# One iteration more between making Z's operands and summing Z, in the attention stage of a fused forward and backward kernel

## The chip, the cores and the metric

The kernel runs on one core of one Trainium2 chip. The metric is device time in microseconds (us) of one execution; the time of a kernel is the median of its runs. The engines are called by the names that the profile uses: PE is TensorE (PEld its weight loads), DVE is VectorE, ACT is ScalarE, POOL is GpSimd, SP is SyncE, whose queue issues most transfers.

## The reference

The kernel computes the output and all gradients of a block with attention and a gated MLP on x of 2048 x 512, with 32 heads of 16:

```python
x = A_x
xn = _layernorm(x, axis=-1)
s = _A_ref(xn, A_wqkv, A_wo)
g = _silu(_B_ref(xn, B_w1, B_b1, B_w2, B_b2))
return x + s * g
```

and in `_A_ref`

```python
scores = jnp.einsum("bhqd,bhkd->bhqk", q, k) * (Dh ** -0.5)
p = _softmax(scores, axis=-1)
o = jnp.einsum("bhqk,bhkd->bhqd", p, v)
```

Outputs are this result and, by `jax.vjp` with a given `grad_out`, the gradients of x, wqkv, wo, w1, b1, w2 and b2. The change lies in the attention stage, where the forward of the softmax and the gradients of q, k and v are made together.

## The kernel before, in words

A first stage (`Pre`) computes the layer norms, the projections and the MLP. The attention stage (`attention_core`) follows, then the rest of the gradients (`Grads.run`). The order of instructions on every engine is written out by hand: an engine works in the order in which the code emits to it, and tiles in pools with few buffers add waits.

The attention stage works on 64 blocks, j = 0 to 63: 16 pairs of heads by 4 chunks of 512 queries (`qc`). A block has 16 iterations, one for every 128 keys (`kb`), and the loop variable g counts all 1024 of them. "Iteration 4" is g % 16 == 4. One iteration emits, among others:

- `emit_d` (L1137): for both heads, the product of the output's gradient with v, `d`, into one of three PSUM buffers; `emit_s` (L1115): the scores `s` of the next iteration, into one double bank; `emit_exp` (L1124, ACT): their exponential into `ets`, a ring of 11 places.
- `emit_z(g + ZOFF)` (L1334): four matmuls of Z, the gradients of k and v, of a block whose first pass lies some iterations back.
- `emit_x` (L1232, L1235, L1239): three groups of four matmuls into X, the sums over keys; the group at L1239 reads `gts` of the iteration before.
- `emit_T` (L1192, L1196): transposes of the exponentials of the iteration before into `tT`; `emit_cT` (L1208, ACT) and `emit_cO` (L1215, DVE) copy them to `ek`, the operand of later Z.
- `emit_mult` (L1155, DVE): two products d * exp, one for each head, into `gts`. A gts buffer holds two iterations, so a new one is opened in the even ones. POOL copies one piece of `ets` beside them (L1153). In the odd iterations `emit_dmat` has SP transpose the buffer by DMA into `gk`, the other operand of Z.

When a block has ended, `emit_xs` (L1248, DVE) takes X out in iteration 0 of the next, `emit_XT` transposes it on PE in iterations 1 and 6, `emit_xt` (L1274) and `emit_fin` take it further on DVE and POOL in 2 and 7, and make the weights W of Z. Z of the block then runs through the following 16 iterations, in two halves (`kp`) of eight:

```python
def z_unit(g):
    j = g // 16
    m = g % 8
    return (j, (g % 16) // 8, m if m < 4 else 7 - m, m // 4) if 0 <= j < NB else None
```

The first four of a half read `gk` and W2, the last four `ek` and W1. Each half is summed in one PSUM bank, and after its eighth iteration `emit_acc` (L1346, L1348, DVE) adds it to `acc`; the next half can begin only when that is done. `emit_acc` stands between the two products of an iteration:

```python
for hj in range(2):
    nc.vector.tensor_tensor(out=gts[:, kb % 2, 4 * hj:4 * hj + 4, :], ...)
    if hj == 0:
        emit_xs(g - 1)
        emit_acc(g + ZOFF)
```

At the last query chunk of a pair POOL casts acc to `ob` (L1352) and issues its two stores (L1355). After the last block the loop goes on for -ZOFF iterations in which only Z is left; `tail_mid` puts the first projections of the next stage (L584, L586, L591, L575) into the third and fourth of them.

Of the kernel before, what the change touches and what calls it, by code (L numbers as in the profile page):

```python
# [1050 lines left out]
def attention_core(ctx, ctx_r, tc, k, grads, Oall, dQall, dKVT_out, ident_f32, ident_bf, npairs=16, nqc=4):  # L1051
# [67 lines left out]
    def emit_exp(g):  # L1119

        a = a_unit(g)
        if a is None:
            return
        nc.scalar.activation(out=st_et[g].rearrange("k b h q -> k h b q"),  # L1124
                             in_=cur["s"][:].rearrange("k h (b q) -> k h b q", b=4), func=ACT.Exp)
# [15 lines left out]
    def emit_mult(g):  # L1141
        a = a_unit(g)
        if a is None:
            emit_xs(g - 1)
            emit_acc(g + ZOFF)
            return
# [7 lines left out]
        for hj in range(2):  # L1154
# [3 lines left out]
# [4 lines that stand above are left out]
# [55 lines left out]
    def emit_x(g, part):  # L1217
        a = a_unit(g)
        if a is None:
            return  # L1220
        j, kb = a
        if part == "e" and kb == 0:
            blk[j]["X"] = ps_x.tile([128, 512], f32, name="X", tag="X")
        X = blk[j]["X"]
        NATt = op_of(j)["NAT"]
        et = st_et[g]
        for c in range(4):
            half, hj = c // 2, c % 2
            r = 32 * c
            ev = et[:, half::2, hj, :]  # L1230
            if part == "e":
                nc.tensor.matmul(X[r:r + 32, 0:256], lhsT=NATt[:, kb, hj, 1:33], rhs=ev,  # L1232
                                 start=(kb == 0), stop=False, skip_group_check=True, tile_position=(0, r))
            elif part == "l":
                nc.tensor.matmul(X[r:r + 32, 256:512], lhsT=Lc[:], rhs=ev,  # L1235
                                 start=False, stop=False, skip_group_check=True, tile_position=(0, r))
            else:
                gv = st_gt[g][:, kb % 2, 4 * hj + half:4 * hj + 4:2, :]
                nc.tensor.matmul(X[r:r + 17, 256:512], lhsT=NATt[:, kb, hj, 0:17], rhs=gv,  # L1239
                                 start=False, stop=(kb == 15), skip_group_check=True, tile_position=(0, r))  # L1240

    def emit_xs(g):
        a = a_unit(g)
        if a is None or a[1] != 15:
            return
        j = a[0]
        xs = xsp.tile([128, 512], f32, name="xs", tag="xs")
        nc.vector.tensor_copy(out=xs[:], in_=blk[j].pop("X")[:])  # L1248
        blk[j]["xs"] = xs
# [66 lines left out]
    def emit_z(g):  # L1316
        u = z_unit(g)
        if u is None:
            return
        j, kp, qb, part = u  # L1320
        if part == 0 and qb == 0:
            blk[j]["Z"] = ps_z.tile([128, 512], f32, name="Z", tag="z")
        Z = blk[j]["Z"]
        for par in range(2):
            kc = 2 * kp + par
            for hj in range(2):
                r = 64 * par + 32 * hj
                if part == 0:
                    mv = blk[j]["Gk"][kc][:, :, 4 * hj + qb, :]
                elif 2 * qb + hj == 7 * (1 - par):  # L1330
                    mv = blk[j]["Gk"][kc][:, :, 8, :]
                else:
                    mv = blk[j]["Ek"][kc][:, :, 2 * qb + hj - par, :]
                nc.tensor.matmul(Z[r:r + 32, :], lhsT=WT[j % 2][1 - part][:, qb, hj, :], rhs=mv,  # L1334
                                 start=(part == 0 and qb == 0), stop=(part == 1 and qb == 0), tile_position=(0, r))

    def emit_acc(g):
        u = z_unit(g)
        if u is None or u[2] != 0 or u[3] != 1:
            return  # L1340
        j, kp = u[0], u[1]
        p, qc = blocks[j]
        Z = blk[j]["Z"]
        av = acc[:, kp, :]
        if qc == 0:
            nc.vector.tensor_copy(out=av, in_=Z[:])  # L1346
        else:
            nc.vector.tensor_tensor(out=av, in0=Z[:], in1=av, op=ALU.add)  # L1348
        if qc == nqc - 1:
            ob = (outp.tile([128, 512], bf16, name="ob") if kp == 0 or j < NB - 1 else  # L1350
                  xsp.tile([128, 512], bf16, name="ob", tag="xs"))
            nc.gpsimd.tensor_copy(out=ob[:], in_=av)  # L1352
            dv = dKVT_out[p * 64:(p + 1) * 64, :].rearrange("r (a b s) -> r a b s", a=2, b=2)
            for b in range(2):
                nc.gpsimd.dma_start(out=dv[:, kp, b, :], in_=ob[b * 64:(b + 1) * 64, :])  # L1355

    FIN_AT = {1: 1, 6: 0}
    FIN_END = {1: 1, 2: 0}
    ZOFF = -20
    late = []  # L1360
    for hj in range(2):
        emit_s(0, hj)
    emit_exp(0)
    for g in range(NSTEP - ZOFF):
        cur["g"] = g
# [20 lines left out]
        emit_exp(g + 1)  # L1386
        emit_z(g + ZOFF)
        emit_x(g - 1, "e")
# [28 lines left out]
def full_kernel(ctx, tc, A_x, A_wqkv, A_wo, B_x, B_w1, B_b1, B_w2, B_b2, grad_out,  # L1417
# [35 lines left out]
    with ExitStack() as cO, tc.manual_schedule():  # L1453
        op0p = cO.enter_context(tc.tile_pool(name="op0", bufs=1, side="right", reuse_waits="tile"))
        k.op0 = make_op(nc, op0p, 0)
        k.Lc = op0p.tile([128, 32], bf16, name="Lc")
        nc.gpsimd.memset(k.Lc[:], 0.0)
        nc.gpsimd.memset(k.Lc[:, 17:18], 1.0)
        op0p.tile([128, 96], mybir.dt.uint8, name="pad_to_256r")
        kv, nat, q, do, natd = op_loads(k, k.op0, 0, nc.sync.dma_start)  # L1460
        first = dict(kv=kv, q=lambda: (nat(), q()), do=lambda g: (do(g * 512, g * 512 + 512), natd(g * 4, g * 4 + 4)))
        with ExitStack() as cP:
            Pre(cP, tc, k, first, A_x, A_wqkv, A_wo, B_w1, B_b1, B_w2, B_b2, grad_out)
        pO = cO.enter_context(tc.tile_pool(name="persistO", bufs=1, reuse_waits="tile"))
        k.Oall = pO.tile([128, NT, D], bf16, name="Oall", tag="Oall")
        k.dQall = pO.tile([128, NT, D], bf16, name="dQall", tag="dQall")
        grads = Grads(cO, tc, k, pO, op0p, A_x, grad_out, A_wqkv, A_wo, B_w1, B_w2,
                      (out_0, out_1, out_2, out_3, out_4, out_5, out_6, out_7))
        with ExitStack() as cB:
            attention_core(cB, cB.enter_context(ExitStack()), tc, k, grads, k.Oall, k.dQall, k.dKVT_s, k.ident_f, k.ident_bf)  # L1470
        grads.run()
# [56 lines left out]
```

## Time and profile before

| what | value |
|---|---|
| median of 3 runs | 2180.5 us (2179.21 to 2181.51) |
| profiled execution, time | 2180.46 us |
| profiled execution, span | 2178.8 us |
| granted TensorE clock, mean | 0.997 |
| busy: PE, DVE, ACT, POOL | 2133.0, 1898.0, 1782.2, 870.6 us |
| products of d and exp (L1155, DVE) | 2048, 682 ns each |
| exponentials (L1124, ACT) | 1024, 1027 ns each |
| sums of Z (L1348 and L1346, DVE) | 96 and 32, 681 ns each |
| Z matmuls (L1334, PE) | 4096, 389 ns each |

Time is counted in the profile from the start of the span. The attention stage takes from about 218 to 1841 us. Four matmuls of one group that go to different parts of the array run side by side, so their durations are not to be added; their starts tell more than their ends.

### The profile page before, as it was taken

How to read it: one execution, taken by the hardware profiler on the slowest of the kernel's cores; microseconds unless marked ns; L12 is line 12 of the kernel's file. 1: busy time of each engine (PE TensorE's matmuls, PEld its weight loads, DVE VectorE, ACT ScalarE, POOL GpSimd, SP SyncE). 2: the span in 40 equal slices, each digit the busy share in tenths (PEclk: the TensorE clock that was granted, in tenths of full speed). 3: DMA queues.
4: the chain of work that ended last, by engine and by line, in shares of the span. 5: the costliest groups of instructions: out<-in, count | busy, mean ns of one | idle time of the engine just before them, and what ended most of it. 6: DMA issues, size and time to landing. Idle time of an engine off the chain costs nothing.

```text
span 2178.8 us, 74934 instructions
## 1 busy us (share of the span) xinstructions
PE 2133.0 (98%) x30659; PEld 1170.6 (54%) x30659; DVE 1898.0 (87%) x3523; ACT 1782.2 (82%) x2481; POOL 870.6 (40%) x2397
## 2 busy tenths in 40 slices
PE   6999999999999999999999999999999999899999
PEld 3444555555555555555555555555555555444444
DVE  6677899999999999999999999999999998788647
ACT  5664899999999999999999999999999997775224
POOL 4376434343434444343434344444434343511003
PEclk9999999999999999999999999999999999999999
DMA  7786999999999999999999999999999999999975
GB/s 235 248 281 202 205 199 198 209 195 200 208 204 198 209 201 201 202 200 206 203 199 201 202 203 201 204 203 204 200 202 206 194 213 212 294 251 240 246 209 178
DMA packets 1416569, 461.17 MB, mean 212 GB/s; under 512 B 1329118, under 2 KB 1400414, under 8 KB 1416224
## 3 DMA queue, kind: packets, MB, share of 16 engines
q1 hardware_dynamic: 1401920, 425.44, 100.3%
q0 software_dynamic: 12720, 29.37, 4.9%
q8 instruction: 240, 3.93, 0.8%
q10 hardware_dynamic: 1584, 1.57, 0.2%
q14 instruction: 105, 0.86, 0.1%
HBM read 62.79 MB, written 64.75 MB: 59 GB/s over the span
## 4 chain that ended last, share of the span: by engine, by line
PE 94%; DVE 2%; DMA 1%; ACT 1%; POOL 0%; issue 0%; SPq 0%; DVEq 0%; ACTq 0%; POOLq 0%
PE tT L1192 22%; PE Z L1334 15%; PE d L1137 15%; PE X L1239 6%; PE X L1232 5%; PE X L1235 5%; PE s L1115 3%; PE ps_dy L909 2%; PE ps_dw L742 2%; PE ps_dw L983 2%; PE ps_h L352 2%; PE ps_m L367 2%; PE ps_dh L875 2%; PE tT L1266 1%; PE ps_dxa L1027 1%; PE ps_dwkv L827 1%
## 5 line engine op out<-in xcount | busy, mean ns | idle before, releaser
L1155 DVE TENSOR_TENSOR gts<-d,ets 128x512 bf16<-128x512 f32 x2048 | 1302.2, 682 | 18.2 <-PE d L1137 3.9
L1124 ACT ACTIVATE ets<-s 128x1024 bf16<-128x1024 f32 x1024 | 1051.6, 1027 | 15.2 <-PE d L1137 3.9
L1208 ACT COPY ek<-tT 128x448 f32<-128x448 f32 (+1 forms) x1024 | 525.1, 513 | 115.0 <-PE tT L1192 31.3
L1192 PE MATMUL tT<-ident_bf,ets 128*128 128x128 bf16 x6790 | 557.9, 221 | 0.0
L1192 PEld LDWEIGHTS <-ets 128*128 128x128 bf16 x6790 | 382.5, 98 | 210.5 <-issue 195.2
L1137 PE MATMUL d<-QDT,KVT 32*128 32x512 bf16 x2048 | 469.4, 384 | 0.0
L1153 POOL COPY gts<-ets 128x128 bf16<-128x128 bf16 x1024 | 281.6, 297 | 387.5 <-ACT ets L1124 382.7
L1115 PE MATMUL s<-QDT,KVT 32*128 32x512 bf16 x2048 | 401.1, 379 | 2.4 <-ACT ets L1124 2.4
L1334 PE MATMUL Z<-gk,W 128*32 128x512 bf16 x2304 | 302.9, 389 | 1.4 <-DVE acc L1348 1.3
L1239 PE MATMUL X<-gts,NAT 128*17 128x256 bf16 x4096 | 290.6, 273 | 0.0
L1232 PE MATMUL X<-ets,NAT 128*32 128x256 bf16 x4096 | 290.4, 273 | 0.0
L1235 PE MATMUL X<-ets,Lc 128*32 128x256 bf16 x4096 | 290.3, 273 | 0.0
L1334 PEld LDWEIGHTS <-W 128*32 128x32 bf16 x4096 | 105.5, 93 | 238.2 <-issue 225.0
L1137 PEld LDWEIGHTS <-KVT 32*128 32x128 bf16 x2048 | 148.5, 91 | 114.3 <-issue 21.5
L1334 PE MATMUL Z<-ek,W 128*32 128x512 bf16 x1792 | 203.6, 389 | 0.0
L1235 PEld LDWEIGHTS <-Lc 128*32 128x32 bf16 x4096 | 110.1, 97 | 108.6
L1215 DVE COPY ek<-tT 128x64 f32<-128x64 f32 x378 | 84.9, 225 | 89.5 <-ACT ek L1208 76.0
L1404 POOL COPY tick<-gts 1x2 bf16<-1x2 bf16 x205 | 36.0, 175 | 313.5 <-DVE gts L1155 313.5
L1115 PEld LDWEIGHTS <-KVT 32*128 32x128 bf16 x2048 | 142.7, 91 | 12.3 <-issue 6.4
L1239 PEld LDWEIGHTS <-NAT 128*17 128x17 bf16 x4096 | 114.7, 91 | 15.4 <-issue 1.1
L1232 PEld LDWEIGHTS <-NAT 128*32 128x32 bf16 x4096 | 108.8, 96 | 5.1 <-issue 5.1
L1295 POOL TENSOR_TENSOR W<-NATQq,rL 128x128 bf16<-128x128 bf16 x64 | 25.5, 399 | 147.9 <-DVE rL L1294 110.3
(252 smaller groups left out, 2470.4 us busy)
## 6 DMA issues: line engine op xcount, KB each, us to landing
gk<-gts SPq DMA_TRANSPOSE x512, 5.6
H1T_s<-h1r SPq DMA_DIRECT2D x28, 256.0 KB, 4.2
HGT_s<-hgT SPq DMA_DIRECT2D x8, 896.0 KB, 4.5
DH_s<-stg SPq DMA_DIRECT2D x12, 512.0 KB, 3.3
hch<-DH_s SPq DMA_DIRECT2D x12, 512.0 KB, 4.8
gp<-H1T_s SPq DMA_DIRECT2D x9, 512.0 KB, 6.8
out_dram<-ob_w POOLq DMA_DIRECT2D x36, 128.0 KB, 4.6
NAT_s<-NS SPq DMA_DIRECT2D x4, 1056.0 KB, 6.1
```

What stands on the lines that cost most here:

```text
L1115: nc.tensor.matmul(s[:, hj, :], lhsT=op["KVT"][r:r + 32, kb * 128:(kb + 1) * 128], rhs=op["QDT"][r:r + 32, qc * 512:(qc + 1) * 512], start ...
L1124: nc.scalar.activation(out=st_et[g].rearrange("k b h q -> k h b q"), in_=cur["s"][:].rearrange("k h (b q) -> k h b q", b=4), func=ACT.Exp)
L1137: nc.tensor.matmul(d[:], lhsT=op["KVT"][r:r + 32, kb * 128:(kb + 1) * 128], rhs=op["QDT"][r:r + 32, qc * 512:(qc + 1) * 512], start=True, ...
L1153: nc.gpsimd.tensor_copy(out=gts[:, kb % 2, 8, :], in_=st_et[g][:, b // 2, b % 2, :])
L1155: nc.vector.tensor_tensor(out=gts[:, kb % 2, 4 * hj:4 * hj + 4, :], in0=st_d.pop((g, hj))[:].rearrange("k (b q) -> k b q", b=4), in1=st_et ...
L1192: nc.tensor.transpose(tb[:, i - cut(g), :], et[:, b // 2, b % 2, :], ident_bf[:])
L1208: nc.scalar.copy(out=blk[j]["Ek"][kb // 4][:, kb % 4, c:7].rearrange("q i k -> q (i k)").bitcast(f32), in_=st_T[g][:, 0:(7 - c) * 64])
L1215: nc.vector.tensor_copy(out=blk[g // 16]["Ek"][kk // 4][:, kk % 4, i].bitcast(f32), in_=st_T[g][:, 448:512])
L1232: nc.tensor.matmul(X[r:r + 32, 0:256], lhsT=NATt[:, kb, hj, 1:33], rhs=ev, start=(kb == 0), stop=False, skip_group_check=True, tile_positi ...
L1235: nc.tensor.matmul(X[r:r + 32, 256:512], lhsT=Lc[:], rhs=ev, start=False, stop=False, skip_group_check=True, tile_position=(0, r))
L1239: nc.tensor.matmul(X[r:r + 17, 256:512], lhsT=NATt[:, kb, hj, 0:17], rhs=gv, start=False, stop=(kb == 15), skip_group_check=True, tile_pos ...
L1334: nc.tensor.matmul(Z[r:r + 32, :], lhsT=WT[j % 2][1 - part][:, qb, hj, :], rhs=mv, start=(part == 0 and qb == 0), stop=(part == 1 and qb = ...
```

## The change

One constant moves by one:

```diff
     FIN_AT = {1: 1, 6: 0}
     FIN_END = {1: 1, 2: 0}
-    ZOFF = -20
+    ZOFF = -21
     late = []
```

`emit_z(g + ZOFF)` and `emit_acc(g + ZOFF)` then belong to an iteration one later. Z of a block began in iteration 4 of the block after it and begins in 5; its two sums were emitted in iterations 11 and, one block later, 3, and are emitted in 12 and 4. In these iterations the sum stands between the two products as before. The loop has one iteration more at its end. Nothing else in the text of the kernel changes; tiles, buffers and the amount of work are the same.

## The prediction

> **What bounds the kernel now.** I read the page first, then the groups of instructions by line, then the timeline of one block of the attention stage, engine by engine. The page:
>
> ```profile
> PE 2133.0 (98%) x30659; PEld 1170.6 (54%) x30659; DVE 1898.0 (87%) x3523; ACT 1782.2 (82%) x2481; POOL 870.6 (40%) x2397
> DVE  6677899999999999999999999999999998788647
> PE 94%; DVE 2%; DMA 1%; ACT 1%; POOL 0%; issue 0%; SPq 0%; DVEq 0%; ACTq 0%; POOLq 0%
> ```
>
> TensorE is busy 98% of the span and carries 94% of the chain that ended last, so nothing looks left to win from another engine. But matmul ends are modelled, and a matmul held up inside its group of four is not told as idle. What the four engines do to each other has to be read from starts. The groups that matter, from the view of groups by line:
>
> ```profile
> L1155 DVE TENSOR_TENSOR gts<-d,ets 128x512 bf16<-128x512 f32 x2048 | 1302.2, 682 | 18.2 <-PE d L1137 3.9 <-ACT ets L1124 1.1 <-POOL tick L1404 1.0
> L1348 DVE TENSOR_TENSOR acc<-Z,acc 128x512 f32<-128x512 f32 x96 | 65.4, 681 | 2.9 <-PE Z L1334 2.9
> L1352 POOL CAST ob<-acc 128x512 bf16<-128x512 f32 x32 | 19.7, 616 | 27.6 <-DVE acc L1348 27.6
> L1355 POOL DMA_DIRECT2D dKVT_s<-ob x64 | 35.8, 562 | 9.6 <-POOL ob L1352 9.5 <-issue 0.2
> ```
>
> 2048 products are two per iteration, in 1024 iterations. I write D4 for the start of the first d matmul in iteration 4 of a block, m0(4) and m1(4) for its two products, T(5) for the transposes and s(5) for the score matmuls issued in iteration 5, and exp(5) for the exponential issued in iteration 4 and read in 5. Block 31 on TensorE, iterations 4 and 5 and the start of 6 (columns: start, length, line, count):
>
> ```profile
> 1010.80 0.39 PE L1137 MATMUL d<-QDT,KVT 32*128 32x512 bf16 x1
> 1010.84 0.39 PE L1115 MATMUL s<-QDT,KVT 32*128 32x512 bf16 x2
> ...
> 1011.17 0.40 PE L1334 MATMUL Z<-gk,W 128*32 128x512 bf16 x4
> ...
> 1011.61 0.40 PE L1239 MATMUL X<-gts,NAT 128*17 128x256 bf16 x4
> 1011.95 0.56 PE L1192 MATMUL tT<-ident_bf,ets 128*128 128x128 bf16 x7
> 1012.45 0.38 PE L1137 MATMUL d<-QDT,KVT 32*128 32x512 bf16 x1
> 1012.45 0.39 PE L1115 MATMUL s<-QDT,KVT 32*128 32x512 bf16 x2
> ...
> 1012.77 0.40 PE L1334 MATMUL Z<-gk,W 128*32 128x512 bf16 x4
> ...
> 1013.21 0.28 PE L1239 MATMUL X<-gts,NAT 128*17 128x256 bf16 x4
> 1013.43 0.56 PE L1192 MATMUL tT<-ident_bf,ets 128*128 128x128 bf16 x7
> ...
> 1013.98 0.39 PE L1137 MATMUL d<-QDT,KVT 32*128 32x512 bf16 x1
> ```
>
> In iteration 5 the transposes start 0.66 after Z, and the four X matmuls that read gts take 0.28. In iteration 4 they take 0.40 and the transposes start 0.78 after Z: TensorE lost 0.12 inside that group. What it waited for is on VectorE and ScalarE:
>
> ```profile
> 1009.80 0.68 DVE L1155 TENSOR_TENSOR gts<-d,ets 128x512 bf16<-128x512 f32 x1
> 1010.40 0.68 DVE L1348 TENSOR_TENSOR acc<-Z,acc 128x512 f32<-128x512 f32 x1
> 1011.00 0.68 DVE L1155 TENSOR_TENSOR gts<-d,ets 128x512 bf16<-128x512 f32 x1
> ```
>
> ```profile
> 1009.76 1.03 ACT L1124 ACTIVATE ets<-s 128x1024 bf16<-128x1024 f32 x1
> ...
> 1011.33 1.03 ACT L1124 ACTIVATE ets<-s 128x1024 bf16<-128x1024 f32 x1
> ...
> 1012.98 1.03 ACT L1124 ACTIVATE ets<-s 128x1024 bf16<-128x1024 f32 x1
> ...
> 1014.54 1.02 ACT L1124 ACTIVATE ets<-s 128x1024 bf16<-128x1024 f32 x1
> ```
>
> VectorE steps on every 0.60 when it is behind. The sum of Z (acc) stands between the two products of iteration 3, so m1(3) starts at 1011.00, one step later than it could, and X and T of the next iteration wait for it: T(4) starts 1011.95 - 1011.00 = 0.95 after m1(3). ScalarE closes the second ring: exp(4) at 1009.76 ends at 1010.79 and s(4) starts 0.05 later, at 1010.84; and exp starts 0.53 after D (1011.33 - 1010.80, 1012.98 - 1012.45), or 0.48 after s where s is late. An exp, its wait and the next s are 1.03 + 0.05 + 0.48 = 1.56, so a block of 16 can hardly be shorter than 25.0: little is to be had here, and a wait of TensorE is partly made up where the exp would have held s anyway.
>
> **The change part by part.** No work is added or removed: the same matmuls of Z, 64 x 2 sums, casts and stores. Everything that hangs on `ZOFF` goes one iteration later.
>
> *Out of iterations 3 and 11.* Iteration 3 keeps its length: acc(3) delays only T(4). In 4 the 0.12 goes: T(4) at 1011.17 + 0.66 = 1011.83, and with the 0.50 from T to D (1011.95 to 1012.45) D5 is 1012.33 instead of 1012.45.
>
> *Into iteration 4.* VectorE would be free at 1010.40 + 0.60 = 1011.00, but m0(4) has to wait for d(4), and then what counts is how soon after D it starts. In even iterations the product opens a new gts buffer, and in the order of the built program it waits for four things there (PE, a DMA queue, ACT, POOL); in odd ones for two. The trace has both cases with VectorE idle, an even one in iteration 4 of block 1 (where no sum stands in 3) and the odd iteration 5 of block 31:
>
> ```profile
> 251.85 0.38 PE L1137 MATMUL d<-QDT,KVT 32*128 32x512 bf16 x1
> ```
>
> ```profile
> 252.43 1.29 DVE L1155 TENSOR_TENSOR gts<-d,ets 128x512 bf16<-128x512 f32 x2 [0.16 <-POOL gts L1153]
> ```
>
> ```profile
> 1012.93 1.29 DVE L1155 TENSOR_TENSOR gts<-d,ets 128x512 bf16<-128x512 f32 x2
> ```
>
> Even: 0.58 after D. Odd: 1012.93 - 1012.45 = 0.48. I take 0.58, from the same iteration and the same four waits; before the change this is hidden in iteration 4, because VectorE comes there late from the sum. After such an idle time the next start is 0.61 later (1.29 less the 0.68 of one product). So m0(4) = 1010.80 + 0.58 = 1011.38, acc at 1011.99, m1(4) at 1012.59, T(5) = 1013.54. Without the wait T(5) would be at 1013.39 or so (exp(5) ends 1012.36, s 1012.41, Z 0.32 later, T 0.66 after it), so m1 decides. T(5) has one transpose more, 0.55 to the next D (1013.43 to 1013.98): D6 = 1014.09 against 1013.98, **+0.11**. Z(5) needs acc(4), over at 1011.99 + 0.68 = 1012.67, before Z's own 1012.73; if it were late, up to 0.15 would vanish under m1. With 0.48, D6 would be 1013.99, +0.01.
>
> The Trainium skill (VectorE: DVE Perf Modes, "The DRAIN you can't avoid") says of chained VectorE copies that a semaphore costs nothing extra. Taken as a rule for these waits it gives the odd value in the even iteration too; the two rows of this trace are 0.10 apart and speak against it here.
>
> *What stays of it.* Before, s(6) waited for exp(6) until 1012.98 + 1.03 + 0.05 = 1014.06, that is 0.08 after D6. After, it starts with D6 at 1014.09: only 0.03 later. But exp(7) starts 0.53 after D6, at 1014.62 against 1014.54: 0.08 later. From there the delay runs on in turns of 0.03 and 0.08, and iteration 12 gets about 0.08.
>
> *Iterations 12 and 13*, where the same happens with the rows
>
> ```profile
> 1023.39 0.38 PE L1137 MATMUL d<-QDT,KVT 32*128 32x512 bf16 x1
> ...
> 1023.78 0.40 PE L1334 MATMUL Z<-gk,W 128*32 128x512 bf16 x4
> ...
> 1024.49 0.56 PE L1192 MATMUL tT<-ident_bf,ets 128*128 128x128 bf16 x7
> ...
> 1026.55 0.39 PE L1137 MATMUL d<-QDT,KVT 32*128 32x512 bf16 x1
> ```
>
> ```profile
> 1025.53 1.03 ACT L1124 ACTIVATE ets<-s 128x1024 bf16<-128x1024 f32 x1
> ```
>
> T(12) gives back 0.05 (0.71 after Z instead of 0.66), but D12 is at 1023.47, m0(12) at 1024.05, m1(12) at 1025.26, T(13) at 1026.21, D14 at 1026.76 against 1026.55: +0.21. s(14) came at 1025.53 + 1.03 + 0.05 = 1026.61 and now comes with D14, +0.15; exp(15), 0.53 after D14, +0.21. The block ends between the two, **+0.18**. From iteration 14 on the sums are the same as before, so the next block starts with this shift and adds its own.
>
> *Elsewhere in the block.* Z itself is four matmuls in every iteration either way. W is written in iteration 2, read now from 5 instead of 4. SP's gk transposes in 1 and 9 now follow a Z of the same iteration, but they wait for m1 of that iteration anyway, which is later than Z. On POOL the cast of ob waits for the sum; behind it stand its two stores and the copies into gts. That runs one iteration later in 32 places; the copies are read by the gk transposes and by nothing on the ring, so I cost it at nothing. Without that cover it is a cast and two issues, 0.62 + 2 x 0.56 = 1.7, in one place per pair.
>
> *The end of the stage.* The first two projections of the tail are issued at fixed iterations, so one of them goes past the sum:
>
> ```profile
> 1845.99 0.68 DVE L1348 TENSOR_TENSOR acc<-Z,acc 128x512 f32<-128x512 f32 x1
> 1846.59 0.68 DVE L586 TENSOR_TENSOR dm_all<-ps_so,s1g 128x512 bf16<-128x512 f32 x1
> ...
> 1847.18 0.68 DVE L591 TENSOR_TENSOR t<-ps_so,s1g 128x512 f32<-128x512 f32 x1
> ```
>
> ```profile
> 1846.72 0.62 PE L1334 MATMUL Z<-gk,W 128*32 128x512 bf16 x8 [0.29 <-DVE acc L1348]
> ```
>
> The last block's Z waits for this sum, and the two products at 1846.59 and 1847.18 now stand ahead of it: two steps of 0.60, **+1.2**, once.
>
> *The sum.* 62 blocks have both sums: 62 x 0.18 = 11.2, with the tail 12.4. The profiled execution took 2180.46 (span 2178.8), practically the median of 2180.5, so the forecast is 2180.5 + 12.4 = 2193.
>
> **The rivals.** *Both waits of X vanish.* The sums leave the stretch of iterations 0 to 3, where xs, its transposed half and the sum pile up on VectorE, and T(4) and T(12) get their 0.12 and 0.05 back: 62 x 0.17 = 10.5 less the tail's 1.2, 2171. For it: VectorE really is idle before m0(4) after the change. Against it: T(5) is free only if m1(4) starts by 1013.39 - 0.95 = 1012.44, so m0(4) by 1011.23, 0.43 after D; the earliest start in the rows is 0.48. That 0.43 is the point that decides. Chance 0.10.
>
> *The four waits cost no more than two.* If they are worked off before d is ready, m0 starts 0.48 after D: D6 +0.01, D14 at 1026.58, +0.03, at most 0.03 a block and 0.02 on the mean of its two turns: 1.2, with the tail 2.4, 2183. For it stands the rule of the skill named above; against it the row at 252.43. Chance 0.14.
>
> *The exps take nothing up.* Then 0.11 and the second wait's own 0.13 stay, 0.24 a block: 14.9 + 1.2, 2197. I hold this for the upper half of the forecast. If POOL's 1.7 came onto the ring in 16 pairs, 27 more; nothing in the waits shows POOL there, 0.03 within the slower cases.
>
> **How the numbers follow.** What a measurement can tell from no change is about 0.2%, 4.4 us. Slower by more: the forecast with its upper case, 0.76. Within: 0.14. Faster: 0.10. The forecast's own range is 2188 to 2199; to hold 8 in 10 it reaches down to 2182, taking in most of the second rival, and up to 2203 for a larger share of the delay.
>
> **What would show it.** Right: in an iteration 5 the X matmuls on gts long (0.4 or more) and T 0.8 after Z, the same in 13; none in 4 and 12; m0(4) and m0(12) 0.58 after D behind an idle VectorE; blocks about 0.18 longer; in the tail Z some 1.2 later behind acc. Wrong: m0(4) at 0.48 or earlier, or T(5) 0.66 after Z.

## Result and profile after

The changed kernel takes 2192.59 us, the median of 6 runs (2190.12 to 2198.02), beside 2180.85 (2177.54 to 2182.04) for 6 runs of the kernel before. The ratio is 1.0059, 95% interval 1.0045 to 1.0073: 11.7 us slower between the medians. A ratio, here and below, is estimated from all runs of both kernels and can differ a little from that of the two medians. The profiled execution after took 2194.41 us, span 2192.7.

The page after, TensorE's share and the two groups that answer to those of before:

```profile
PE 2148.5 (98%) x30659; PEld 1175.7 (54%) x30659; DVE 1896.9 (87%) x3523; ACT 1786.7 (81%) x2481; POOL 870.6 (40%) x2397
L1155 DVE TENSOR_TENSOR gts<-d,ets 128x512 bf16<-128x512 f32 x2048 | 1302.6, 683 | 52.1 <-POOL gts L1153 20.4
L1239 PE MATMUL X<-gts,NAT 128*17 128x256 bf16 x4096 | 296.4, 273 | 0.0
```

Every engine has the same instructions as before; a page alone would say that TensorE became busier by 15 us. The second line tells more: VectorE stands idle before the products for 52.1 us instead of 18.2. The view of VectorE's waits within the attention stage puts the new ones down as follows (us in total, times, longest):

```profile
DVE gts L1155 <- POOL gts L1153: 20.4, 61, 0.3
DVE gts L1155 <- PE s L1115: 18.3, 60, 0.3
```

About 60 times each, that is once a block: the first is m0(12), the second m0(4). In the list of before each of them stands once, with 0.2 us, because VectorE came to these two products late there. The name behind the arrow is that of the semaphore event that came last, which need not be what held the product: before m0(12) POOL's copy ends 0.38 after D (median), earlier than VectorE is done with waiting for d (0.43, see below). The timeline of block 31 on TensorE, iterations 4 and 5, then 12 and 13, with the start of the iteration behind (block 30 started at 986.90 and block 31 at 1012.32):

```profile
986.90 0.38 PE L1137 MATMUL d<-QDT,KVT 32*128 32x512 bf16 x1
...
1012.32 0.38 PE L1137 MATMUL d<-QDT,KVT 32*128 32x512 bf16 x1
...
1018.67 0.38 PE L1137 MATMUL d<-QDT,KVT 32*128 32x512 bf16 x1
...
1019.02 0.39 PE L1334 MATMUL Z<-ek,W 128*32 128x512 bf16 x2
...
1019.47 0.28 PE L1239 MATMUL X<-gts,NAT 128*17 128x256 bf16 x4
1019.68 0.56 PE L1192 MATMUL tT<-ident_bf,ets 128*128 128x128 bf16 x7
1020.18 0.39 PE L1137 MATMUL d<-QDT,KVT 32*128 32x512 bf16 x1
...
1020.61 0.40 PE L1334 MATMUL Z<-gk,W 128*32 128x512 bf16 x4
...
1021.05 0.43 PE L1239 MATMUL X<-gts,NAT 128*17 128x256 bf16 x4
1021.42 0.56 PE L1192 MATMUL tT<-ident_bf,ets 128*128 128x128 bf16 x7
...
1021.97 0.39 PE L1137 MATMUL d<-QDT,KVT 32*128 32x512 bf16 x1
1021.97 0.39 PE L1115 MATMUL s<-QDT,KVT 32*128 32x512 bf16 x2
...
1031.36 0.38 PE L1137 MATMUL d<-QDT,KVT 32*128 32x512 bf16 x1
...
1033.31 0.40 PE L1334 MATMUL Z<-gk,W 128*32 128x512 bf16 x4
...
1034.10 0.56 PE L1192 MATMUL tT<-ident_bf,ets 128*128 128x128 bf16 x7
...
1034.65 0.39 PE L1137 MATMUL d<-QDT,KVT 32*128 32x512 bf16 x1
```

VectorE in the same block (the bracket is the idle time ahead and who ended it):

```profile
1019.26 0.69 DVE L1155 TENSOR_TENSOR gts<-d,ets 128x512 bf16<-128x512 f32 x1 [0.31 <-PE s L1115]
1019.87 0.68 DVE L1348 TENSOR_TENSOR acc<-Z,acc 128x512 f32<-128x512 f32 x1
1020.47 1.88 DVE L1155 TENSOR_TENSOR gts<-d,ets 128x512 bf16<-128x512 f32 x3
...
1031.94 0.69 DVE L1155 TENSOR_TENSOR gts<-d,ets 128x512 bf16<-128x512 f32 x1 [0.34 <-POOL gts L1153]
```

The X group in iteration 4 is back at 0.28 and T follows Z by 0.66 there; in iteration 5 X takes 0.43 and T follows Z by 0.81, in iteration 13 by 0.79. The wait of X has not gone, it has moved one iteration on and grown.

Medians over all blocks, from D to the next D in ns (columns are iterations of a block):

| | 0 | 3 | 4 | 5 | 6 | 7 | 12 | 13 | 14 | 15 | block, us |
|---|---|---|---|---|---|---|---|---|---|---|---|
| before | 1596 | 1570 | 1646 | 1538 | 1614 | 1550 | 1602 | 1556 | 1594 | 1504 | 25.220 |
| after | 1552 | 1584 | 1510 | 1789 | 1538 | 1612 | 1550 | 1734 | 1537 | 1558 | 25.423 |

The block length is that of the third query chunk. There the difference is 0.20; in the other chunks it is 0.20 to 0.22, except in the first chunk of every second pair, where it is 0.08 (25.582 against 25.499). The mean over the 62 blocks is 0.19. From the start of block 1 to the start of block 63 the attention stage is 12.0 us longer in the one profiled execution than in the other, 1581.2 against 1569.2 us. The difference of the medians is in the blocks.

### The profile page after: what moved, and what is told of

It reads as the page before. It is cut to its first block, busy times and chain, and to the rows that moved or that the text cites. A ratio compares the mean times of both kernels' runs of the same rounds, so it can differ in the third digit from the quotient of the medians.

```text
span 2192.7 us, 75058 instructions
## 1 busy us (share of the span) xinstructions
PE 2148.5 (98%) x30659; PEld 1175.7 (54%) x30659; DVE 1896.9 (87%) x3523; ACT 1786.7 (81%) x2481; POOL 870.6 (40%) x2397
## 3 DMA queue, kind: packets, MB, share of 16 engines
q10 hardware_dynamic: 1584, 1.57, 0.2%
## 4 chain that ended last, share of the span: by engine, by line
PE 93%; DVE 2%; DMA 2%; ACT 1%; SPq 1%; POOL 0%; issue 0%; DVEq 0%; ACTq 0%; POOLq 0%
PE tT L1192 22%; PE d L1137 15%; PE Z L1334 15%; PE X L1239 6%; PE X L1232 5%; PE X L1235 5%; PE s L1115 3%; PE ps_dy L909 2%; PE ps_dw L983 2%; PE ps_dw L742 2%; PE ps_h L352 2%; PE ps_m L367 2%; PE ps_dh L875 2%; PE tT L1266 1%; PE ps_qkv L210 1%; PE ps_dxa L1027 1%
## 5 line engine op out<-in xcount | busy, mean ns | idle before, releaser
L1155 DVE TENSOR_TENSOR gts<-d,ets 128x512 bf16<-128x512 f32 x2048 | 1302.6, 683 | 52.1 <-POOL gts L1153 20.4
L1137 PE MATMUL d<-QDT,KVT 32*128 32x512 bf16 x2048 | 475.5, 384 | 0.0
L1239 PE MATMUL X<-gts,NAT 128*17 128x256 bf16 x4096 | 296.4, 273 | 0.0
L1137 PEld LDWEIGHTS <-KVT 32*128 32x128 bf16 x2048 | 152.7, 90 | 114.3 <-issue 21.4
L1115 PEld LDWEIGHTS <-KVT 32*128 32x128 bf16 x2048 | 147.1, 90 | 13.8 <-issue 5.1
```

What stands on the lines that cost most here:

```text
L1115: nc.tensor.matmul(s[:, hj, :], lhsT=op["KVT"][r:r + 32, kb * 128:(kb + 1) * 128], rhs=op["QDT"][r:r + 32, qc * 512:(qc + 1) * 512], start ...
L1137: nc.tensor.matmul(d[:], lhsT=op["KVT"][r:r + 32, kb * 128:(kb + 1) * 128], rhs=op["QDT"][r:r + 32, qc * 512:(qc + 1) * 512], start=True, ...
```

## The experiments

The theory: in iterations 4 and 12 the product m0 is no longer hidden behind a late VectorE, and its four waits, worked off one after another once d is there, set its start; acc, m1, T and the next D follow at fixed distances. The rivals: the sum of Z costs what it costs wherever it stands with VectorE's time in the iteration (then the four waits do not matter); or something other than the sums, which hangs on the same constant, makes the difference.

**The waits taken off the product (first_touch).** A tiny write into the new gts buffer takes over the waits for the buffer's earlier readers and can be worked off while d is still being computed:

```diff
         nc.gpsimd.tensor_copy(out=gts[:, kb % 2, 8, :], ...)
+        if kb in (4, 12):
+            nc.vector.memset(gts[:, 0, 0, 0:1], 0.0)
         for hj in range(2):
```

> The changed kernel with one tiny VectorE write (128x1) into the new gts buffer ahead of the first product of iterations 4 and 12, so that the waits for POOL and the transposes are worked off while VectorE is idle, and the product waits for PE and ACT alone. Theory (the four waits set when the product starts): m0(4) and m0(12) start about 0.49 after D instead of 0.59, T(5) and T(13) each 0.10 earlier, blocks 0.15 to 0.20 shorter, 2181 to 2184. Rival (the place of the sum sets it, whatever it waits for): m0 stays at 0.58, 2192 to 2193.

It took 2182.64 us (2176.63 to 2185.94) beside 2179.23 for the kernel before: ratio 1.0009, interval 0.9998 to 1.0019, clear of the 1.0045 to 1.0073 of the change alone. Block 30 on TensorE, its start, its iteration 4, and the start of block 31 (lines behind the new statement are shifted by two):

```profile
980.93 0.38 PE L1137 MATMUL d<-QDT,KVT 32*128 32x512 bf16 x1
...
987.28 0.38 PE L1137 MATMUL d<-QDT,KVT 32*128 32x512 bf16 x1
...
989.22 0.40 PE L1336 MATMUL Z<-gk,W 128*32 128x512 bf16 x4
...
1006.15 0.38 PE L1137 MATMUL d<-QDT,KVT 32*128 32x512 bf16 x1
```

and on VectorE:

```profile
987.52 0.06 DVE L1155 MEMSET gts<- 128x1 bf16 x1
987.76 0.69 DVE L1157 TENSOR_TENSOR gts<-d,ets 128x512 bf16<-128x512 f32 x1 [0.19 <-PE s L1115]
988.37 0.68 DVE L1348 COPY acc<-Z 128x512 f32<-128x512 f32 x1
988.97 1.28 DVE L1157 TENSOR_TENSOR gts<-d,ets 128x512 bf16<-128x512 f32 x2
```

With one instruction *more* on VectorE, m0(4) starts 0.48 after D instead of 0.59, iteration 5 is 1679 ns instead of 1789, iteration 13 is 1636 instead of 1734, and the block is 1006.15 - 980.93 = 25.22 long, as before the change. The trace also records VectorE's own semaphore instructions, which the page does not count as busy. Ahead of m0(4), medians over the blocks in ns after D:

| | first ends | second starts | second ends | product starts |
|---|---|---|---|---|
| after | 447 | 495 | 545 | 589 |
| first_touch | 434 | none | none | 478 |

The product starts 44 ns behind the last of them in both. In the changed kernel the first waits for PE alone and ends 0.45 after D; the second waits for a DMA queue and ACT, the product itself for POOL. The exponential (ACT) is over 0.02 before D and POOL's copy 0.34 after it, so the waits for these two are met before the first instruction ends. The second instruction still runs for 50 ns, and with the gap ahead of it costs 98 ns, all of it on the way to m0. Ahead of m0(12) the changed kernel has two as well: the first, which waits for d, ends at 433, the second at 531, and the product follows at 575. Over the whole execution VectorE has 1425 such instructions in the changed kernel and 1299 here, 126 fewer, which is two in each of 63 blocks. The Trainium skill (Perfetto Trace Analysis, "Identifying Dependency Chains") says that an instruction which waits for several engines may get semaphore instructions ahead of it. The trace agrees, and adds a price: 98 ns for one of them that stands behind the last arrival on an idle engine.

**Most sums left out, with both constants (few_after, few_before).** If something other than the sums hangs on the constant, the two stay apart.

```diff
-        if qc == 0:
+        if qc == nqc - 1:
             nc.vector.tensor_copy(out=av, in_=Z[:])
-        else:
-            nc.vector.tensor_tensor(out=av, in0=Z[:], in1=av, op=ALU.add)
```

> The changed kernel with three of four sums of Z left out (only the sum of the last query chunk of a pair is made, as a copy, so dK and dV hold one chunk alone). Theory (the sum between the products is all that costs): 46 of 62 blocks lose the 0.20 that the change brought and a few hundredths more, 2178 to 2181, within 1.5 of the kernel before with the same sums left out. Rival (something else that hangs on the constant costs: Z beside eight transposes in 5 and 13, SP's or POOL's waits): it stays 6 to 12 above that kernel.

> The kernel before with three of four sums of Z left out (dK and dV hold one chunk alone). 96 sums of 0.68 go, 65 us of VectorE. Theory (the ring of s and exp takes up most of a wait of TensorE): at most 0.05 to 0.10 in 46 blocks, 2176 to 2179. Rival (VectorE's load or the waits of 0.12 and 0.05 are fully on the path): 46 x 0.17 = 8, 2173 or below.

2177.96 us (ratio 0.9995, 0.9985 to 1.0004) and 2177.84 (0.9994, 0.9983 to 1.0005): the same, as far as runs can tell that spread over 10 us. Block 30, which has no sum in either, on TensorE with the constant of after

```profile
981.32 0.38 PE L1137 MATMUL d<-QDT,KVT 32*128 32x512 bf16 x1
...
1006.46 0.38 PE L1137 MATMUL d<-QDT,KVT 32*128 32x512 bf16 x1
```

and with that of before:

```profile
979.01 0.38 PE L1137 MATMUL d<-QDT,KVT 32*128 32x512 bf16 x1
...
1004.16 0.38 PE L1137 MATMUL d<-QDT,KVT 32*128 32x512 bf16 x1
```

25.14 and 25.15. The blocks that keep one of the two sums differ. Where it stands in 4 or 3, they take 25.297 against 25.227 in one half of the pairs and 25.333 against 25.229 in the other. Where it stands in 12 or 11, they take 25.326 against 25.200 in one half, but 25.434 against 25.450 in the other, so the constant costs nothing there; why has not been followed. By these lengths the constant is still worth 2.3 us in this pair of kernels, less than the medians resolve. So the constant costs only through the sums. The pair shows two things more. In few_before, in the blocks without a sum, m0(4) starts 0.59 and m0(12) 0.58 after D, as in the changed kernel: what brings the late start out is not the constant but that VectorE is idle; without a sum behind it, it costs T nothing. And with the constant of before, both sums together lengthen a block by 25.220 - 25.147 = 0.07. The 65 us of VectorE that were left out were worth 1.4 us between the medians (2.9 by the lengths of all kinds of block), because nearly all of it lay beside TensorE.

**The reader of the late product put off (defer_after).** X on gts is read one iteration later in 5 and 13, so T(5) no longer waits for m1(4).

```diff
-        if g % 16 == 2:
+        if g % 16 in (2, 6, 14):
             emit_x(g - 2, "g")
-        if g % 16 != 1:
+        if g % 16 not in (1, 5, 13):
             emit_x(g - 1, "g")
```

> The changed kernel with the X matmuls that read the delayed products moved on by one iteration: none in 5 and 13, eight in 6 and 14 (as the kernel has it in 1 and 2). Theory: T(5) and T(13) no longer wait, but iterations 6 and 14 get 0.11 longer and the exps hold s in 5 and 13, so only some 0.10 to 0.17 of a block comes back: 2182 to 2187. Rival (a wait of TensorE counts in full): 0.18 + 0.13 a block, 2173.

2186.48 us (2180.65 to 2188.71), ratio 1.0031, 1.002 to 1.0042: about half of the loss is back. Block 30, iterations 5 and 6 on TensorE:

```profile
990.27 0.38 PE L1137 MATMUL d<-QDT,KVT 32*128 32x512 bf16 x1
...
991.80 0.39 PE L1137 MATMUL d<-QDT,KVT 32*128 32x512 bf16 x1
...
992.69 0.39 PE L1239 MATMUL X<-gts,NAT 128*17 128x256 bf16 x8
```

Iteration 5 falls to 1.53 (median 1522 ns), the eight X matmuls make 6 long (1771), and the block of the third chunk is 25.294, 0.13 shorter than after. The wait did sit in X of 5 and 13. Why 0.08 of the block stays has not been followed.

**The same delay put in on purpose (dose_after, dose_before).** A one-column copy out of d stands ahead of the products in 4 and 12.

```diff
+        if kb in (4, 12):
+            nc.vector.tensor_copy(out=gts[:, 0, 0, 0:1], in_=st_d[g, 0][:, 0:1])
         for hj in range(2):
```

> The changed kernel with a tiny VectorE copy of one column of d ahead of the first product of iterations 4 and 12; it waits for d and the product waits for it. This adds to the suspected cost. Theory (every delay of m0 there goes through m1 into T(5) and T(13)): m0 starts 0.08 to 0.15 later than 0.59, blocks 0.15 to 0.28 longer, 2201 to 2210. Rival (the exps or another ring cover it): 2192 to 2195.

> The kernel before with the same tiny copy in the same iterations 4 and 12. Theory: there VectorE comes late from the sum of 3 and 11, m0(4) moves from 0.80 to about 0.95 and m1(4) still is 0.1 ahead of what T(5) needs, so nothing is lost: 2179 to 2183. Rival (any delay of VectorE in 4 and 12 costs the same): 9 to 17 more, 2189 to 2198.

With the constant of after, 2222.93 us (2221.69 to 2224.15), ratio 1.0187, 1.0171 to 1.0202. VectorE in iteration 4 of block 30, where D was at 1004.86:

```profile
1005.33 0.16 DVE L1155 CAST gts<-d 128x1 bf16<-128x1 f32 x1 [0.19 <-POOL gts L1153]
1005.60 0.69 DVE L1157 TENSOR_TENSOR gts<-d,ets 128x512 bf16<-128x512 f32 x1
```

m0(4) starts 0.74 after D, 0.154 later than in the changed kernel, m0(12) 0.167 later, and the blocks of the third chunk are 0.32 longer: the two delays arrive whole. With first_touch (0.111 and 0.097 earlier, block 0.206 shorter) that is a straight line through three points. The first chunk gives the same 0.32 in every second pair and 0.22 in the others. The blocks of the other two chunks are longer by a further 0.35, which neither theory had. With the constant of before it is there too, and the waits of VectorE name it:

```profile
DVE gts L1157 <- POOL tick L1406: 11.9, 30, 0.4
```

In every second block a product of iteration 0 now waits for POOL's tick (12.2 us in 30 waits with the constant of after; less these, its time is 2210.7, just above the upper end of what was expected). That is a side effect of the extra instruction, and I take it off: 11.9 us of the 19.2 by which dose_before (2200.61, 2196.91 to 2203.93; ratio 1.0084, 1.007 to 1.0098) stands above its kernel before. What is left, some 7 us, and 0.15 in the blocks of the third chunk, which have no side effect, is not what I expected: I had held that VectorE's lateness before m0(4) swallows the copy. The time is nearer to that of the rival (9 to 17), but not by its reason, that a delay costs the same with either constant: m0(4) and m0(12) move by 0.26 and 0.21 here, and only 0.15 of it arrives. VectorE's lateness does not swallow the copy, as iteration 4 with the start of 5 shows, first on VectorE, then on TensorE:

```profile
996.72 0.15 DVE L1155 CAST gts<-d 128x1 bf16<-128x1 f32 x1
996.98 1.89 DVE L1157 TENSOR_TENSOR gts<-d,ets 128x512 bf16<-128x512 f32 x3
```

```profile
997.57 0.38 PE L1137 MATMUL d<-QDT,KVT 32*128 32x512 bf16 x1
997.58 0.39 PE L1115 MATMUL s<-QDT,KVT 32*128 32x512 bf16 x2
997.72 0.37 PE L1137 MATMUL d<-QDT,KVT 32*128 32x512 bf16 x1
998.02 0.40 PE L1336 MATMUL Z<-gk,W 128*32 128x512 bf16 x4
```

D4 was at 995.92, so m0(4) has gone from 0.80 to 1.06 after D. The second d of iteration 5 then starts 0.15 behind the first, where otherwise it starts 0.01 behind it, and Z moves with it. m0(4) ends at 996.98 + 0.68 = 997.66, 0.06 ahead of that second d: I read this as the wait for the bank of d that m0(4) sets free, which no further run took apart. In the kernel before, m0(4) then has hardly any slack toward that bank. So the expectation fell, through a second route from m0 to TensorE.

**The sum behind both products (sum_last).** If the cost is only m1 being late, putting acc after m1 saves it; if Z of the next half needs acc at once, it costs more.

```diff
             if hj == 0:
                 emit_xs(g - 1)
-                emit_acc(g + ZOFF)
+        emit_acc(g + ZOFF)
```

> The changed kernel with the sum behind both products of its iteration instead of between them. Theory: m1(4) is then early and X on gts does not wait, but Z(5) needs the bank that the sum empties: the sum ends about 2.48 after D4, Z(5) starts about 0.6 later than now, which takes the place of the wait of 0.18: blocks 0.8 to 0.9 longer than in the changed kernel, 2242 to 2248. Rival (only the delay of the second product costs): 0.2 a block less, 2180.

2248.96 us (2248.16 to 2249.76), ratio 1.0306, 1.0288 to 1.0325, a little above what was expected. TensorE at iteration 5 of block 31:

```profile
1019.12 0.38 PE L1137 MATMUL d<-QDT,KVT 32*128 32x512 bf16 x1
...
1020.14 0.40 PE L1334 MATMUL Z<-gk,W 128*32 128x512 bf16 x4 [0.52 <-DVE acc L1346]
```

Z starts 1.02 after D and TensorE is told as idle for 0.52. Z is 0.59 later than in the changed kernel, where it starts 0.43 after D: one step of VectorE. The place between the products is the cheaper one, since a late m1 costs T 0.15 and a late acc costs Z a whole step; blocks of the third chunk are 0.89 longer than after.

**The end of the stage (touch_tail).** first_touch, with the two projections one step later in the tail:

```diff
-        if n == 2:
+        if n == 3:
             self.emit_so(0)
...
-        if n == 3:
+        if n == 4:
             self.emit_so(1)
```

> The changed kernel with the tiny write ahead of the product (as in first_touch) and the tail's first two projections one iteration later, so that no product of a projection stands ahead of the sum that the last block's Z waits for. Theory: the tail gets 1.2 back: 2178 to 2182, as fast as the kernel before within 0.2%. Rival (the 1.2 is taken up later in the tail anyway): the same as first_touch, 2181 to 2184.

2184.41 us (2178.39 to 2188.69), ratio 1.0014, 1.0003 to 1.0024: no gain on first_touch is seen, but intervals of this width cannot tell 1.2 us. The step itself did move: from the end of the last product to the third projection are 12.17 us in the changed kernel and 11.14 here (10.70 before). Whether that reaches the end of the kernel stays open. From the end of the last product to the start of the later `ps_dh` (L875) the profiled executions have 146.25 us before, 146.14 after, 148.53 in first_touch and 145.24 here; after and first_touch have the same tail, and differ by 2.4.

**X behind the transposes (x_behind_after, x_behind_before).** The X group on gts is emitted behind T, in the iterations in which it waits, so that T goes ahead of the wait. The diff is that of x_behind_after; with the constant of before the iterations are 4 and 12.

```diff
-        if g % 16 != 1:
+        if g % 16 not in (1,) + (5, 13):
             emit_x(g - 1, "g")
         st_T.pop(g - 2, None)
         emit_T(g - 1)
+        if g % 16 in (5, 13):
+            emit_x(g - 1, "g")
```

> The changed kernel with the four X matmuls that read the delayed products put behind the transposes in iterations 5 and 13, so that TensorE has work while it waits. Theory (only the order on TensorE makes the delayed product count): no wait is left, T and the copy to ek come 0.11 earlier; the price is one more change between the kinds of matmul, 0 to 0.2 in two iterations of a block. Blocks 25.15 to 25.35, 2177 to 2188. Rival (the delayed product costs by another way, the d banks as in dose_before): 25.4 as now, 2191 to 2194.

> The kernel before with the same, in iterations 4 and 12. Theory: its waits of 0.12 and 0.05 go, the same price: blocks 25.15 to 25.30, 2176 to 2185; if the price is near nothing this beats both kernels by about 4.

2185.01 us (2182.87 to 2189.85), ratio 1.0026, 1.0016 to 1.0036; and 2179.29 (2174.08 to 2185.62), 0.9999, 0.9987 to 1.0011. For the constant of after, TensorE at the end of iteration 5:

```profile
991.18 0.29 PE L1239 MATMUL X<-gts,NAT 128*17 128x256 bf16 x4
991.40 0.38 PE L1137 MATMUL d<-QDT,KVT 32*128 32x512 bf16 x1
```

Behind T the group holds the next D for 0.22, twice the 0.11 between the starts of the X groups where they follow each other, so half of the gain goes into the place behind T, which I read as one more change between kinds of matmul: blocks of the third chunk are 0.11 shorter than after, not 0.21. With the constant of before, where the wait is only 0.12 and 0.05, that price takes all of it, and nothing is left to win. No version that does all the work ran faster than the kernel before.

## Why the prediction was right

The time was forecast at 2193.0 and is 2192.59, and the steps came out as follows.

- *Out of iterations 3 and 11*: the 0.12 went. Iteration 4 is 136 ns shorter, 12 is 52.
- *m0(4) at 0.58 after D*: 0.59, and m0(12) 0.58, both behind an idle VectorE. The reading of the built program's four waits held, and first_touch showed that they are the cause and not merely beside it. acc came 0.61 later and m1 0.60 after that, as in the chain of the forecast.
- *T(5) 0.95 after m1*: 1021.42 - 1020.47 = 0.95. *D6 +0.11*: iterations 4 and 5 together are 1510 + 1789 - 1646 - 1538 = 115 ns longer.
- *What stays of it*: s(6) starts with D6 (both 1021.97), no longer behind it, as forecast. Iterations 6 to 11 together give back 15 ns, so iteration 12 gets 0.10 where 0.08 was forecast.
- *Iterations 12 and 13, D14 +0.21*: 126 ns of their own, 0.226 with what was carried.
- *Block end +0.18*: 0.20 in the table, 0.19 in the mean of the 62 blocks. This term was a little too small. The forecast let the exponentials take up 0.06 of 0.24; in the table 0.115 and 0.126 come to 0.24 too, and all other iterations together take up 0.04.
- *62 blocks, 11.2*: 12.0 in the stage of the profiled execution, and 11.7 between the medians, whose interval is 9.8 to 15.9.
- *The tail, 1.2*: right at its place, but not seen in the time. VectorE and TensorE there:

```profile
1861.14 0.68 DVE L591 TENSOR_TENSOR t<-ps_so,s1g 128x512 f32<-128x512 f32 x1
1861.74 0.68 DVE L1348 TENSOR_TENSOR acc<-Z,acc 128x512 f32<-128x512 f32 x1
```

```profile
1862.47 1.05 PE L1334 MATMUL Z<-gk,W 128*32 128x512 bf16 x16 [1.43 <-DVE acc L1348]
```

acc does stand behind the two products of the projection, and Z is told as idle for 1.43 instead of 0.29, 1.1 more. But from the end of the last product to the start of the later `ps_dh` are 146.25 us before and 146.14 after, so in this pair of executions nothing of it is left there. With a spread of 2.4 between executions, the runs do not show whether the term was put onto a path that had slack behind it. That it happened to make up for the block term being 0.8 too small is luck.

The rivals. *Both waits of X vanish* (2171) fell at its own point: it needed m0(4) by 0.43 after D, and even without the second semaphore instruction (first_touch) it starts at 0.48. *Four waits cost no more than two* (2183) is refuted for the changed kernel, and first_touch, which makes it true by hand, ran at 2182.64, its forecast time. The rule that stood for it, of the Trainium skill (VectorE: DVE Perf Modes, "The DRAIN you can't avoid"), that a semaphore costs nothing extra, was said of chained copies. Where VectorE is idle and waits for the last of several engines, the runs show 0.10 us for the second semaphore instruction, in 4 as in 12. *The exps take nothing up* (2197) did not hold: the block's 0.19 to 0.20 lies nearer to the forecast's 0.18 than to this rival's 0.24. *POOL's 1.7* did not come: the blocks in which POOL casts, those of the first two chunks, grew by 0.08 to 0.22, the others by 0.20.

Left open: moving the sums on into the odd iterations 5 and 13, where the product has only two waits, was not tried. With the six buffers that there are, gk would be taken again in iteration 9 before Z has read it for the last time in 10.

## What to carry to other kernels

Before an instruction is moved to a place where its engine seems to have time, look at what that engine's lateness was hiding there: here an instruction that came late had its waits worked off under the one before it, and one that came early paid for those behind the last arrival. A wait that has to stay can be given to a tiny instruction ahead, which touches the same buffer and runs while the last operand is still being made. And a full engine is not a price list: 65 us of VectorE were worth 1 to 3 us here, and 0.1 us at the wrong place, twice in a block, 12 us.

## What the runs showed of the hardware that was not expected

A second semaphore instruction, behind the one that waited for d, held VectorE's product back by 98 ns, gap included. The size had been forecast from two rows; that a single instruction makes it had not. Under a VectorE that is still busy the same two cost nothing: in iteration 4 of the kernel before they end 0.54 after D, and the product follows the one before it by the usual 0.60, at 0.80. Moving four X matmuls behind the transposes cost 0.22 us instead of the 0.11 that they take among their kind. And a one-column copy on VectorE, 0.15 us, opened a wait for POOL in another iteration, 0.4 us in every second block, 11.9 in all: an instruction put in as a dose can cost elsewhere, and its side effect has to be found in the waits before its result is read.
